# Loads tied in the planner to the up projection also wait for it on the chip

## The chip, the cores and the metric

The kernel runs on one core of one Trainium2 chip. The metric is device time in microseconds (us) of one execution, the median of several.

## What is computed

Two layers, one after the other. The first is a cross-covariance attention over channels: q and k (4 batches, 6208 rows, 256 channels) are normalised along the rows, `kn^T qn` gives a 256 x 256 matrix for each batch, and its softmax multiplies v. The second is a channel mix with a squared relu and a gate.

```python
def _attn_ref(q, k, v, tau):
    qn = q / (np.linalg.norm(q, axis=1, keepdims=True) + 1e-06)
    kn = k / (np.linalg.norm(k, axis=1, keepdims=True) + 1e-06)
    s = kn.transpose(0, 2, 1) @ qn / tau
    a = np.exp(s - s.max(-1, keepdims=True))
    a /= a.sum(-1, keepdims=True) + 1e-09
    return v @ a

def _moe_ref(x, mu_k, mu_r, w_k, w_v, w_r):
    x_prev = np.concatenate([zeros, x[:, :-1, :]], axis=1)
    xk = mu_k * x + (1.0 - mu_k) * x_prev
    xr = mu_r * x + (1.0 - mu_r) * x_prev
    k = np.maximum(xk @ w_k, 0.0)
    v = k * k @ w_v
    r = 1.0 / (1.0 + np.exp(-(xr @ w_r)))
    return r * v
```

Inputs and output are float32; the kernel multiplies in bfloat16.

## The kernel before, in words

**Blocks.** The rows are cut into 48 blocks of 512 (12 for each batch) and one block "left" of the 4 x 64 rows that remain; the constant T = 9.6 us is the planned time of a block. Around the blocks of batch b - 1 the kernel gathers the covariance of batch b: 12 groups of 512 rows of q and k and one small group of 64 rows (32 KB for each of q and k). Only the first batch's covariance comes before all blocks, in a head of some 45 us.

**One block.** A load on POOL's queue brings v as bfloat16 (L394, "ld v"; six buffers `v_bf`); SP's queue turns it with a transposing DMA (L400; six buffers `vT`), or, for the first five blocks, TensorE does. TensorE makes x from `vT` and the softmaxed matrix `A` (L489), ACT takes it out of PSUM into `xR` (L501), and DVE makes `xk` and `xr` (L533, L540, L549). The up projection is four *pairs* (L578): each pair is two planner steps called "up", with two matmuls of 512 columns in each; ACT's relu (L581) and DVE's square (L583) take the pair on. The gate (L611) and the down projection (L616) go to PSUM `vr`, ACT's tanh (L620) and DVE's product (L622) write `res`, of which there are three buffers, and SP stores 512 KB (L636).

**One group of the next covariance.** Two loads on POOL's queue bring q and k (L676, "ld qk"; 13 buffers `qk`); ACT squares them (L691), DVE adds the squares up (L694 to L704), TensorE multiplies (L714). At the end of a batch stand the sums of the squares (L724, L731), a power step on POOL (L277), a chain of small DVE steps (L279 to L296, with matmuls at L302) and the softmax (L433 to L454).

**What sets the order.** Nothing is scheduled by the compiler: `Plan` holds every step with its engine, a cost, a key and the steps it depends on, and `order()` runs a list schedule with these costs. The steps are then emitted in the planned order, and each engine and queue keeps that order on the chip. What an instruction waits for on the chip is set by the tiles that it reads and writes.

**The pace of the loads.** Near the end of the kernel all loads of v and of q and k are sorted by when they are used, and spread at four for each T, at most 3 T ahead of their use. `after_pair(t)` finds the up pair planned for that time:

```python
def after_pair(t):
    at = [m for m in [marks.get((n, p)) for n, p in [divmod(int((t + T) / T * 4), 4)]] if m]
    return at
```

The second "up" step of a pair is its mark (`marks[n, p]`, set in `up_pair`). The load takes the mark as `after=`, and `add` puts it among the load's dependencies. That holds in the planner's time alone: load and matmul share no tile, so on the chip the load waits for its buffer to come free, for one of the DMA queue's semaphores, and for the instructions before it on POOL. Besides the loads, POOL's queue holds a small memset of `xR` at the start of each batch (L473) and the power steps (L277).

Of the kernel before, what the change touches and what calls it, by code (L numbers as in the profile page):

```python
# [15 lines left out]


class Step:
    __slots__ = ("eng", "occ", "lat", "out", "key", "fn", "deps", "users", "left", "ready", "start", "seq", "size", "name", "take", "give")


class Plan:

# [10 lines left out]
        self.readers = {}  # L36
        self.fill_from, self.fill_to, self.fill, self.fill_stop = 0.0, 0.0, None, ()

    def add(self, eng, cost, key, fn, reads=(), writes=(), size=0, name="", after=(), take=None, give=None):
        s = Step()  # L40
        s.occ, s.lat = cost if isinstance(cost, tuple) else (cost, cost)
        s.eng, s.key, s.fn, s.size, s.name = eng, key, fn, size, name
        s.seq = len(self.steps)
        s.take, s.give = take, give
        s.deps, s.users = set(after), []
        for r in reads:
            if r in self.writer:
                s.deps.add(self.writer[r])
            self.readers.setdefault(r, []).append(s)
        for w in writes:  # L50
            if w in self.writer:
                s.deps.add(self.writer[w])
            for r in self.readers.get(w, ()):
                s.deps.add(r)
            self.writer[w] = s
            self.readers[w] = []
        s.deps.discard(s)
        self.steps.append(s)
        return s

    def order(self):
        import heapq
        for s in self.steps:
            s.left = len(s.deps)
            s.ready = 0.0
            for d in s.deps:
                d.users.append(s)
        free = {e: 0.0 for e in self.HOP}
        waiting = {e: [] for e in self.HOP}
        able = {e: [] for e in self.HOP}  # L70
        lanes = {"SP": [], "POOL": []}
        bus = {"SP": 0.0, "POOL": 0.0}
        for s in self.steps:
            if s.left == 0:
                heapq.heappush(waiting[s.eng], (0.0, s.seq, s))
        done = []
        held, queued, open_at = set(), {}, {}
        while True:
            best = None
            for e in free:  # L80
                if able[e]:
                    t = free[e]
                elif waiting[e]:
                    t = max(free[e], waiting[e][0][0])
                else:
                    continue
                if best is None or t < best[0]:
                    best = (t, e)
            if best is None:
                break  # L90
            t, e = best
            if e == "PE" and self.fill and free[e] < self.fill_to and t > self.fill_from and t - free[e] > 0.3:
                at = max(free[e], self.fill_from)
                n = min(512, int((t - at - 0.05) * 2400) // 64 * 64)
                if n >= 64:
                    f = Step()
                    f.eng, f.occ, f.lat = "PE", n / 2400 + 0.0025, n / 2400
                    f.start, f.seq, f.name, f.fn = at, 0, "fill", (lambda n=n: self.fill(n))
                    f.deps, f.users, f.key, f.size, f.out = set(), [], 0, 0, at + f.lat
                    f.take = f.give = None  # L100
                    done.append(f)
                    free[e] = at + f.occ
                    continue
            while waiting[e] and waiting[e][0][0] <= t:
                _, q, s = heapq.heappop(waiting[e])
                heapq.heappush(able[e], (s.key, q, s))
            s = heapq.heappop(able[e])[2]
            if s.take:
                if s.take in held:
                    queued.setdefault(s.take, []).append(s)  # L110
                    continue
                if open_at.get(s.take, 0.0) > t + 1e-9:
                    heapq.heappush(waiting[e], (open_at[s.take], s.seq, s))
                    continue
                held.add(s.take)
            if s.size:
                lane = lanes[e][-8] + 0.25 if len(lanes[e]) >= 8 else 0.0
                if lane > t + 1e-9:
                    heapq.heappush(waiting[e], (lane, s.seq, s))
                    continue  # L120
            s.start = t
            if s.name in self.fill_stop:
                self.fill_to = 0.0
            free[e] = t + s.occ
            end = t + s.lat
            if s.size:
                at, took = max(bus[e], end + self.MOVE), s.size / self.RATE
                if e == "SP" and bus["POOL"] > at:
                    bus["POOL"] += took
                    took *= 4 if s.name == "turn v" else 2  # L130
                bus[e] = at + took
                end = bus[e] + self.LAND
                lanes[e].append(end)
                if t > self.SPARE_FROM:
                    end += self.SPARE
            s.out = end
            if s.give:
                held.discard(s.give)
                open_at[s.give] = end + self.HOP["PE"]
                for w in queued.pop(s.give, ()):  # L140
                    heapq.heappush(waiting[w.eng], (max(w.ready, open_at[s.give]), w.seq, w))
            done.append(s)
            for u in s.users:
                r = free[e] if u.eng == e and not s.size else end + self.HOP[u.eng]
                u.ready = max(u.ready, r)
                u.left -= 1
                if u.left == 0:
                    heapq.heappush(waiting[u.eng], (u.ready, u.seq, u))
        done.sort(key=lambda s: (s.start, s.seq))
        return done  # L150
# [18 lines left out]
def kernel(  # L169
# [104 lines left out]
    def inverse(i, key, srcn, sres, lo, hi, name):  # L274

        nres = ("nq" if lo == 0 else "nk", i)
        add("POOL", (0.8, 0.9), key + .01, lambda: nc.gpsimd.tensor_tensor(nrm[i][:, lo:hi], srcn[:, lo:hi], half[:, lo:hi], op=OP.pow),  # L277
            reads=[(sres, i)], writes=[nres], name=name + " pow")
        add("DVE", TINY, key + .02, lambda: nc.vector.tensor_scalar_add(nrm[i][:, lo:hi], nrm[i][:, lo:hi], 1e-6),  # L279
            reads=[nres], writes=[nres], name=name)  # L280
        rw = [("rrq", i)] if hi == 2 else [("rrk", i)] if lo == 2 else [("rrq", i), ("rrk", i)]
        add("DVE", TINY, key + .03, lambda: nc.vector.reciprocal(rr[i][:, lo:hi], nrm[i][:, lo:hi]),
            reads=[nres], writes=rw, name=name)
        if inv_tau != 1.0 and hi == 4:
            add("DVE", TINY, key + .03, lambda: nc.vector.tensor_scalar_mul(rr[i][:, 2:4], rr[i][:, 2:4], inv_tau),
                reads=[("rrk", i)], writes=[("rrk", i)], name=name)
# [101 lines left out]
    head_last = plan.steps[-1]  # L388


    def v_load(n, key, after=()):
        b, t = blocks[n]
        i = n % NV
        add("POOL", 0.75, key, lambda: nc.gpsimd.dma_start(  # L394
            v_bf[i], v[b, t * M:(t + 1) * M, :].rearrange("(s p) c -> p s c", p=P)),
            writes=[("v_bf", i)], size=M * C * 4, name="ld v", after=after)

    def v_turn_dma(n, key):
        i, o = n % NV, n % NT
# [168 lines left out]
    def up_pair(n, p, c0, c1, w, ku):  # L568
        def go():
# [3 lines left out]
            for x in range(2):  # L573
                fh = 2 * p + x

                def mm(fh=fh, x=x):
                    for dh in range(2):
                        nc.tensor.matmul(kT[bk][:, x, :w], w_k[:, dh, fh * P:(fh + 1) * P], xk[n % 2][:, dh, c0:c1],  # L578
                                         start=dh == 0, stop=dh == 1)
                marks[n, p] = add("PE", pe(w, 2), ku + x * .02, mm, reads=[("w_k",), ("xk", n % 2, c0)], writes=[("kT", bk, x)], name="up")  # L580
            add("ACT", act(2 * w), ku + .1, lambda: nc.scalar.activation(kr[kri][:, :, :w], kT[bk][:, :, :w], AF.Relu, scale=0.5 ** 0.5),  # L581
                reads=[("kT", bk, 0), ("kT", bk, 1)], writes=[("kr", kri)], name="relu")
# [64 lines left out]
    def left_stage(b, key):  # L647
        i = b % 2
        unit(key, lambda: add("POOL", 0.6, key, lambda: nc.gpsimd.dma_start(vl[i][:80], v[b, N - 80:, :]),
                              writes=[("vl", i)], size=80 * C * 4, name="ld v", after=[marks[NB * b + 1, 3]]))  # L650
        unit(key + .1, lambda: add("SP", 1.2, key + T, lambda: nc.sync.dma_start_transpose(vlT[i], vl[i][:80, :]),
                                   reads=[("vl", i)], writes=[("vlT", i)], size=80 * C * 4, name="turn v"))

# [16 lines left out]
    def qk_load(b, g, key, pace):  # L670
# [3 lines left out]
        G = qk[gi]  # L674
        for x, t in enumerate((q, k)):
            add("POOL", 0.55, key + x * .001, lambda x=x, t=t: nc.gpsimd.dma_start(G[:rows, x, :n], src(t, b, g)),  # L676
                writes=[("qk", gi, x, j) for j in range(S)], size=rows * n * C * 4, name="ld qk", after=pace(x))

    def cov_group(b, g, key, dk):
        rows, n = (P, S) if g < NB else (L, 1)  # L680
# [142 lines left out]
        fn()  # L823
    seq = plan.order()
    tc_plan[:] = seq
    for s in seq:
        s.fn()


tc_plan = []  # L830
# [38 lines left out]
```

## Time and profile before

| | |
|---|---|
| timed runs | 527.08, 525.74, 523.83 us; median 525.74 |
| the profiled execution's own time | 524.58 us |
| its span, first to last instruction | 522.8 us |
| TensorE busy (PE) | 490.3 us, 94% of the span |
| DVE, ACT, POOL busy | 434.5, 403.4, 102.7 us |
| moved by DMA | 77.36 MB; HBM read 78.71 MB, written 25.43 MB |
| median from issue to landing, v / k / q loads | 9.3 / 10.3 / 10.3 us |
| median from issue to landing, stores / transposes | 4.3 / 6.8 us |

How to read the lines that follow. PE is TensorE's matmuls, PEld its weight loads, DVE VectorE, ACT ScalarE, POOL GpSimd, SP SyncE; SPq is SP's sequencer, which issues transfers. L578 is line 578 of the kernel. In a row of the timeline the first two numbers are start and duration in us, and a bracket tells how long the engine was idle before it and what ended that. A row of a 10 us stretch gives the busy time of PE, PEld, DVE, ACT and POOL, each with its instructions, then the granted TensorE clock, the DMA share and the GB/s moved. A row of the waits names who waited, for whom, the total in us, how many times, and the longest. A row of the DMA issues ends with the median time from issue to landing. The row of digits "DMA" is the busy share of the DMA engines in 40 equal slices of the span, in tenths.

### The profile page before, as it was taken

The page shows a single profiled execution, that of the slowest core. Times are in us where ns is not written, and L with a number is a line of the kernel's source. Part 1 is how long each engine was busy: PE and PEld are TensorE (multiplying, and loading weights), DVE is VectorE, ACT ScalarE, POOL GpSimd, SP SyncE. Part 2 cuts the span into 40 slices and gives each one's busy share as a digit, 9 for nine tenths or more (in the row PEclk, how much of TensorE's full clock was granted, in tenths as well). Part 3 has the DMA queues.
Part 4 walks back from the last instruction along what each step waited for, and adds up shares of the span by engine and source line. Part 5 has one row for each costly group of instructions (what it writes and reads, how often), then busy time and mean ns, then how long its engine had stood idle before and what let it go on. Part 6 is the DMA issues. An engine that isn't in the chain of part 4 may idle for free.

```text
span 522.8 us, 9475 instructions
## 1 busy us (share of the span) xinstructions
PE 490.3 (94%) x3483; PEld 335.4 (64%) x3544; DVE 434.5 (83%) x988; ACT 403.4 (77%) x576; POOL 102.7 (20%) x174
## 2 busy tenths in 40 slices
PE   1889999999999997999999999999999999999995
PEld 0555666666666674666666667676666666666674
DVE  3768999999989995899779989989669787878973
ACT  4956798988888885788878788888666777777763
POOL 6465433100343321100234211000122000000000
PEclk9999999999999999999999999999999999999999
DMA  9999999993899999942699999642399463322213
GB/s 203 209 203 202 190 216 198 201 203 77 147 182 205 184 198 200 189 100 61 121 203 200 216 165 201 113 107 60 83 161 163 101 105 101 81 82 61 81 45 97
DMA packets 113942, 77.36 MB, mean 148 GB/s; under 512 B 49572, under 2 KB 101480, under 8 KB 113896
## 3 DMA queue, kind: packets, MB, share of 16 engines
q0 software_dynamic: 41776, 38.84, 49.4%
q1 hardware_dynamic: 72120, 37.92, 33.7%
q8 instruction: 27, 0.44, 0.3%
q14 instruction: 19, 0.16, 0.1%
HBM read 78.71 MB, written 25.43 MB: 199 GB/s over the span
## 4 chain that ended last, share of the span: by engine, by line
PE 66%; DVE 19%; DMA 8%; ACT 3%; issue 2%; POOL 0%; SPq 0%; ACTq 0%; DVEq 0%; POOLq 0%
PE vr L616 25%; PE kT L578 24%; PE vr L611 6%; PE xp L489 6%; DMA qk<-in_k_dram 5%; PE s_ps L714 4%; DVE kk L583 4%; DMA out_dram<-res 3%; DVE dm L540 3%; DVE res L622 2%; DVE xk L549 1%; DVE t L694 1%; DVE xr L549 1%; DVE dl L533 1%; ACT kr L581 1%
## 5 line engine op out<-in xcount | busy, mean ns | idle before, releaser
L581 ACT ACTIVATE kr<-kT 128x1024 bf16<-128x1024 f32 (+1 forms) x200 | 200.0, 1002 | 55.1 <-PE kT L578 49.9
L616 PE MATMUL vr<-w_v,kk 128*128 128x256 bf16 x1552 | 204.7, 273 | 1.8 <-DVE kk L583 1.5
L578 PE MATMUL kT<-xk,w_k 128*128 128x512 bf16 (+1 forms) x742 | 200.5, 372 | 5.3 <-DVE xk L549 2.1
L583 DVE TENSOR_TENSOR kk<-kr 128x1024 bf16<-128x1024 bf16 (+1 forms) x200 | 133.6, 670 | 43.8 <-ACT kr L581 43.6
L616 PEld LDWEIGHTS <-kk 128*128 128x128 bf16 x1552 | 150.7, 98 | 24.5 <-DVE kk L583 5.2
L578 PEld LDWEIGHTS <-w_k 128*128 128x128 bf16 x800 | 77.3, 98 | 56.5 <-issue 3.5
L620 ACT ACTIVATE res<-vr 128x256 f32<-128x256 f32 x194 | 75.1, 388 | 22.2 <-PE vr L616 13.5
L622 DVE SCALAR_TENSOR_TENSOR res<-res,vr 128x256 f32<-128x256 f32 x194 | 80.1, 414 | 7.0 <-ACT res L620 7.0
L611 PE MATMUL vr<-w_r,xr 128*128 128x256 bf16 x388 | 74.1, 273 | 3.3 <-DVE res L622 3.2
L501 ACT CAST xR<-xp 128x512 bf16<-128x512 f32 x94 | 55.4, 590 | 21.1 <-PE xp L489 20.9
L691 ACT ACTIVATE sq<-qk 128x2048 bf16<-128x2048 bf16 (+1 forms) x39 | 70.7, 1812 | 0.0
L540 DVE TENSOR_SCALAR dm<-dl,mu 128x512 bf16<-128x512 bf16 (+1 forms) x200 | 61.7, 347 | 1.0
L611 PEld LDWEIGHTS <-xr 128*128 128x128 bf16 x388 | 37.6, 98 | 38.1 <-issue 4.7
L394 POOL DMA_DIRECT2D v_bf<-in_v_dram x48 | 36.6, 765 | 110.4 <-DMA vT<-v_bf 55.5
L489 PE MATMUL xp<-vT,A 128*128 128x512 bf16 x188 | 56.1, 379 | 0.7 <-DVE A L454 0.2
L714 PE MATMUL s_ps<-qk 128*128 128x256 bf16 (+1 forms) x294 | 55.1, 273 | 0.5 <-DVE e_sb L433 0.4
L714 PEld LDWEIGHTS <-qk 128*128 128x128 bf16 (+1 forms) x294 | 28.4, 98 | 15.3 <-issue 1.1
L549 DVE TENSOR_TENSOR xk<-dm,xR 128x1024 bf16<-128x1024 bf16 (+1 forms) x49 | 33.4, 682 | 1.7
L549 DVE TENSOR_TENSOR xr<-dm,xR 128x1024 bf16<-128x1024 bf16 (+1 forms) x49 | 33.4, 682 | 1.5
L533 DVE TENSOR_TENSOR dl<-xR 128x1024 bf16<-128x1024 bf16 (+1 forms) x49 | 33.0, 674 | 0.1
L309 ACT ACTIVATE sq<-qk 128x1024 bf16<-128x1024 bf16 (+2 forms) x26 | 24.1, 975 | 9.0 <-DMA qk<-in_q_dram 5.6
L489 PEld LDWEIGHTS <-A 128*128 128x128 bf16 x196 | 19.1, 98 | 18.4 <-DVE A L454 1.3
(81 smaller groups left out, 251.1 us busy)
## 6 DMA issues: line engine op xcount, KB each, us to landing
out_dram<-res SPq DMA_DIRECT2D x47, 512.0 KB, 4.3
v_bf<-in_v_dram POOLq DMA_DIRECT2D x48, 256.0 KB, 9.3
qk<-in_k_dram POOLq DMA_DIRECT2D x47, 256.0 KB, 10.3
qk<-in_q_dram POOLq DMA_DIRECT2D x46, 256.0 KB, 10.3
f32s<-in_q_dram SPq DMA_DIRECT2D x2, 512.0 KB, 4.2
vT<-v_bf SPq DMA_TRANSPOSE x43, 6.8
w_k<-in_moe_w_k_dram POOLq DMA_DIRECT2D x1, 512.0 KB, 7.0
w_v<-in_moe_w_v_dram POOLq DMA_DIRECT2D x1, 512.0 KB, 8.8
```

The source lines that it names most:

```text
L489: nc.tensor.matmul(dst, A[b][:, ih, dh * P:(dh + 1) * P], vT[o].rearrange("p (s h) q -> p h s q", h=2)[:, ih, c0 // P:c1 // P, :], start=i ...
L540: unit(km, lambda col=col, dh=dh, c0=c0, c1=c1, km=km, w=w: add("DVE", dve(w, 2.77), km, lambda: nc.vector.tensor_scalar_mul(dm[di][:, dh, ...
L549: nc.vector.tensor_tensor(o[which][:, :, c0:c1], dm[di][:, :, c0:c1], xR[:, :, at + c0:at + c1], op=OP.add)
L578: nc.tensor.matmul(kT[bk][:, x, :w], w_k[:, dh, fh * P:(fh + 1) * P], xk[n % 2][:, dh, c0:c1], start=dh == 0, stop=dh == 1)
L581: add("ACT", act(2 * w), ku + .1, lambda: nc.scalar.activation(kr[kri][:, :, :w], kT[bk][:, :, :w], AF.Relu, scale=0.5 ** 0.5), reads=[("k ...
L583: add("DVE", dve(2 * w, 2), ku + .2, lambda: nc.vector.tensor_tensor(kk[n % 2][:, 2 * p:2 * p + 2, c0:c1], kr[kri][:, :, :w], kr[kri][:, : ...
L611: nc.tensor.matmul(V[:, D:], xr[ri][:, dh, s * P:(s + 1) * P], w_r[:, dh, :], start=dh == 0, stop=dh == 1)
L616: nc.tensor.matmul(V[:, :D], kk[n % 2][:, fh, s * P:(s + 1) * P], w_v[:, fh, :], start=fh == 0, stop=fh == 7)
L620: add("ACT", act(D), kd + .3, lambda: nc.scalar.activation(r[:, s], V[:, D:], AF.Tanh, scale=0.5), reads=[("vr", bk)], writes=[("res", oi, ...
L622: add("DVE", dve(D), kd + .4, lambda: nc.vector.scalar_tensor_tensor(r[:, s], r[:, s], 1.0, V[:, :D], op0=OP.add, op1=OP.mult), reads=[("v ...
L691: add("ACT", act(w), key, lambda: nc.scalar.activation(Q[:rows, :, :n], G[:rows, :, :n], AF.Square), reads=both, writes=sqs, name="sq")
L714: nc.tensor.matmul(s_ps[:, ih, :], G[:rows, 1, s, ih * P:(ih + 1) * P], G[:rows, 0, s, :], start=g == 0 and s == 0 and ih == 0, stop=g == ...
```

## The change

The loads of v (of blocks and of the left rows) and of q and k hand their mark over as `gate=` in place of `after=`. For the planner this is the same dependency. When the program is emitted, each load also gets a real dependency on the last matmul of the marked up step, which becomes a wait on a semaphore of TensorE. To have that matmul at hand, a step keeps the instruction that its function returns, and `mm` returns its last matmul. Apart from that, the planner's cost of the power step goes from 0.8 us (0.9 until its result is there) to 1.0 (1.1).

```diff
-    def add(self, eng, cost, key, fn, reads=(), writes=(), size=0, name="", after=(), take=None, give=None):
+    def add(self, eng, cost, key, fn, reads=(), writes=(), size=0, name="", after=(), take=None, give=None, gate=()):
...
-        s.take, s.give = take, give
-        s.deps, s.users = set(after), []
+        s.take, s.give, s.gate, s.inst = take, give, gate, None
+        s.deps, s.users = set(after) | set(gate), []
...
-        add("POOL", (0.8, 0.9), key + .01, lambda: nc.gpsimd.tensor_tensor(nrm[i][:, lo:hi], srcn[:, lo:hi], half[:, lo:hi], op=OP.pow),
+        add("POOL", (1.0, 1.1), key + .01, lambda: nc.gpsimd.tensor_tensor(nrm[i][:, lo:hi], srcn[:, lo:hi], half[:, lo:hi], op=OP.pow),
...
-    def v_load(n, key, after=()):
+    def v_load(n, key, gate=()):
...
-            writes=[("v_bf", i)], size=M * C * 4, name="ld v", after=after)
+            writes=[("v_bf", i)], size=M * C * 4, name="ld v", gate=gate)
...
                 def mm(fh=fh, x=x):
                     for dh in range(2):
-                        nc.tensor.matmul(kT[bk][:, x, :w], w_k[:, dh, fh * P:(fh + 1) * P], xk[n % 2][:, dh, c0:c1],
-                                         start=dh == 0, stop=dh == 1)
+                        last = nc.tensor.matmul(kT[bk][:, x, :w], w_k[:, dh, fh * P:(fh + 1) * P], xk[n % 2][:, dh, c0:c1],
+                                                start=dh == 0, stop=dh == 1)
+                    return last
...
-                              writes=[("vl", i)], size=80 * C * 4, name="ld v", after=[marks[NB * b + 1, 3]]))
+                              writes=[("vl", i)], size=80 * C * 4, name="ld v", gate=[marks[NB * b + 1, 3]]))
...
-                writes=[("qk", gi, x, j) for j in range(S)], size=rows * n * C * 4, name="ld qk", after=pace(x))
+                writes=[("qk", gi, x, j) for j in range(S)], size=rows * n * C * 4, name="ld qk", gate=pace(x))
...
+    wait = mybir.DependencyInfo(mybir.DependencyClass.Sync, mybir.DependencyReason.DATA)
     for s in seq:
-        s.fn()
+        s.inst = s.fn()
+        for g in s.gate:
+            tc.add_manual_dep(s.inst.ins, g.inst.ins.name, wait, reason="pace")
```

More of the change, by code (lines that the diff above doesn't have):

```diff
@@ L18 @@
 class Step:
-    __slots__ = ("eng", "occ", "lat", "out", "key", "fn", "deps", "users", "left", "ready", "start", "seq", "size", "name", "take", "give")
+    __slots__ = ("eng", "occ", "lat", "out", "key", "fn", "deps", "users", "left", "ready", "start", "seq", "size", "name", "take", "give", "gate", "inst")
 class Plan:
@@ L99, in order @@
                     f.deps, f.users, f.key, f.size, f.out = set(), [], 0, 0, at + f.lat
-                    f.take = f.give = None
+                    f.take, f.give, f.gate, f.inst = None, None, (), None
                     done.append(f)
```

## The prediction

> **What bounds the kernel now.** I read the page's busy shares and slices first, then the stretches of 10 us, then the waits and queues where a stretch falls short.
>
> ```profile
> span 522.8 us, 9475 instructions
> PE 490.3 (94%) x3483; PEld 335.4 (64%) x3544; DVE 434.5 (83%) x988; ACT 403.4 (77%) x576; POOL 102.7 (20%) x174
> PEclk9999999999999999999999999999999999999999
> DMA  9999999993899999942699999642399463322213
> ...
> 190.00:200.00 10.00, 9.81 (x70) 6.79 (x70) 6.83 (x15) 5.44 (x7) 1.81 (x3) 1.00 1.23 178
> 200.00:210.00 10.00, 6.68 (x46) 4.45 (x47) 7.71 (x17) 8.03 (x12) 1.86 (x4) 1.00 1.44 210
> 210.00:220.00 10.00, 9.89 (x70) 6.86 (x70) 9.06 (x21) 8.28 (x12) 1.81 (x3) 1.00 1.22 188
> ```
>
> TensorE is the bound: the clock is granted in full, and from 50 to 510 us nearly every stretch of 10 us has 9.8 to 9.95 us of matmul. So a change of transfers can win only what is missing there. The largest hole is 200 to 210 (6.68 us). The waits from 190 to 212 name it, and SP's timeline shows where it begins:
>
> ```profile
> ACT res L620 <- DMA out_dram<-res: 4.4, 1, 4.4
> DVE res L622 <- ACT res L620: 3.8, 1, 3.8
> PE vr L611 <- DVE res L622: 2.2, 2, 1.4
> ...
> 182.69 0.54 SPq L636 DMA_DIRECT2D out_dram<-res  x1
> 183.33 10.97 SPq L400 DMA_TRANSPOSE vT<-v_bf  x1
> 219.61 1.72 SPq L400 DMA_TRANSPOSE vT<-v_bf  x1
> ```
>
> The store issued at 182.69 landed at 200.31 (its landing event). Three `res` buffers go round, so ACT's tanh of the block three further on waited 4.4 us for it; DVE and TensorE stood behind. A transpose holds SP 10.97 us there and 1.72 us in a calm stretch. The cause is on POOL's queue, of whose rows these matter:
>
> ```profile
> 90.05 0.64 POOL L676 DMA_DIRECT2D qk<-in_k_dram  x1 [0.44 <-DMA qk<-in_k_dram]
> 184.26 0.53 POOL L676 DMA_DIRECT2D qk<-in_k_dram  x1 [0.51 <-DMA v_bf<-in_v_dram]
> 211.25 0.56 POOL L676 DMA_DIRECT2D qk<-in_k_dram  x1
> 255.52 0.11 POOL L473 MEMSET xR<- 128x2 bf16 x1 [43.72 <-DVE xr L549]
> 270.01 1.04 POOL L277 TENSOR_TENSOR nrm<-acc,half 128x4 f32<-128x4 f32 x1 [10.88 <-DVE acc L731]
> ```
>
> I paired the planner's order of before with the trace's rows, engine by engine (both keep one order), and so know for each load the up pair that the plan ties it to. Of 124 tied loads 123 are issued before that pair ends, by 24 us on average and 46 at most: the load at 184.26 belongs behind the pair that ends at 227.65, the one at 211.25 behind 252.07. The loads run in bursts until buffers are full, and POOL then stands 43.72 us. What the bursts do to the queues, as issues and median time to landing, first for 150 to 186, then for 203 to 212, then for 420 to 521:
>
> ```profile
> qk<-in_k_dram POOLq DMA_DIRECT2D x9, 256.0 KB, 13.8
> out_dram<-res SPq DMA_DIRECT2D x3, 512.0 KB, 16.1
> ...
> v_bf<-in_v_dram POOLq DMA_DIRECT2D x2, 256.0 KB, 8.1
> qk<-in_k_dram POOLq DMA_DIRECT2D x2, 256.0 KB, 10.5
> ...
> out_dram<-res SPq DMA_DIRECT2D x11, 512.0 KB, 2.9
> v_bf<-in_v_dram POOLq DMA_DIRECT2D x1, 256.0 KB, 4.1
> vT<-v_bf SPq DMA_TRANSPOSE x5, 3.9
> ```
>
> **The change, part by part.**
>
> *The wait itself.* 124 loads now wait on POOL for TensorE. Up matmuls already signal ACT's relu, so TensorE gets no instruction. The hop: the relu at 185.35 starts 0.03 us after the modelled end of its matmuls (184.29 + 1.03), so I take 0.3 us as its upper bound. It makes each load 0.3 us later at most, which is held against the room of the loads below. Price by itself 0, as POOL is 20% busy.
>
> *What stands behind the waiting load on POOL.* Three memsets and three power steps. The memsets at 255.52 and 375.24 follow loads tied to pairs ending at 252.07 and 366.67, long before DVE releases them; the one at 131.77 follows 130.97, and 130.97 + 0.3 + 0.75 = 132.0 makes it 0.3 us late for a column that is read by the first delta of the next batch, a full 28 us behind it in the plan. The power at 150.31 follows a load freed at 149.14 (149.14 + 0.3 + 0.59 = 150.0: in time). The one at 270.01 follows a load freed at 269.38: 269.38 + 0.3 + 0.58 = 270.3, so up to 0.3 us late. The third follows 386.00 and runs at 389.39: in time. A softmax chain hangs on each power, with TensorE gaps around it; so +0.2 us, bounds 0 and 0.6 (twice 0.3).
>
> *Loads issued later.* This is where it can lose. Whoever waits for a q or k load is ACT's square (L691), in ACT's order, with relu and tanh behind it. From the end of its pair to that square each of the 35 tied full k loads has 8.9 to 18 us, most 9 to 11; the q loads have 10.9 and more. The load with the tightest room of all, 8.3 us, is a 32 KB remainder. So the question is how long a paced load takes. The bounds: 4.1 us (alone) and 13.8 (deep in the burst). Paced loads come some 2.4 us apart. A load needs 1.3 us of the engines (loads alone in the head move 203 GB/s, 262 KB each), a store with its transpose 3.0 (DMA share 0.30 of 430 to 440, where one of each runs). A block of some 9.5 us with 3.9 loads thus asks 3.9 x 1.3 + 3.0 = 8.1 us, 85%. The nearest row is 203 to 212, where loads come three at once beside a store and a transpose: 8.1 to 10.5. Without the burst two of three stand less in line, 1.3 to 2.6 us less: I take 6 to 8. That is inside 8.9, price 0; with 0.2 us for single late ones: +0.2. At the upper end, all landing in 10.5 as the median load of the whole trace does, the k loads would be late by 18 us in sum (some 20 loads, 0.9 each).
>
> The Trainium skill ("DMA: Bandwidth & Descriptors", section "Rules for kernel authors") speaks against this change: issue a DMA early and wait for it late, so that its fixed cost overlaps. The trace agrees only in part: early loads were never waited for after the head, but their burst held the store of 182.69 for 17.6 us. By the rule alone the change would win nothing and lose what lands late.
>
> *v loads.* They have 2 to 12 us before SP turns to their transpose, and some will hold SP by up to about 4 us. Behind the transpose on SP stands the next store, a block (9 us) later; the transposed tile is used 8 to 44 us after it lands, and with shallower queues it lands sooner than the 13 to 21 us of the bursts. Price 0.
>
> *The stall at 200.* Paced, a store should land in 3 to 8 us, under the 13.3 us (182.69 to 195.98, where ACT began to wait) from which it hurts. The hole goes. Its size: 9.95 - 6.68 = 3.3 us by the stretch; 4.15 by the gaps between weight loads from 199.59 to 209 beyond a matmul's own time (1.58, 0.84, 1.05, 0.68). I take 3.5. What is late next is nothing on the transfer side: the other gaps (0.5 at 61 and 67, 1.4 at 296 to 300, 1.4 at 395 to 399, some 1.6 at 274 to 280) name DVE and ACT.
>
> *The planner's power step, 0.8 to 1.0 us.* The trace has 1.04 to 1.13 for four columns. No row shows DVE waiting for it, so the number saves nothing itself; it can shift the order around three batch boundaries, whose gaps sum to about 4.6 us. Bounds -4.6 and +4.6; I take 0, since the order is kept by keys and the shift is 0.2 us.
>
> *Sum* against the profiled execution: 524.58 us (span 522.8 and 1.8 around it) - 3.5 + 0.2 + 0.2 = 521.4. Its 524.58 is 1.2 under the median of the three timed runs (525.74; 523.83 to 527.08); as queue depth may differ from run to run, I carry half of that: **522.0 us**, 0.7% below the median.
>
> **The rivals.**
>
> *A: paced loads land late (slower).* Place: the square's wait for the k load, 35 times. It decides from a landing of 8.9 us on. At 10.5 us 18 us of lateness, of which half to all reaches TensorE (the one ACT wait for a DMA, 4.4 us, cost 3.3 to 4.2): 521.4 + 9 to 18 = 530 to 540, say 535. For it: the DMA engines are 85% asked for, and 8.1 to 10.5 is the nearest row. Against: there three loads came at once.
>
> *B: no gain.* The store stall returns elsewhere, or the time passes to the next wait, or the wait does not hold since the last reader of the buffer is later anyway. For it: only one store stall shows in 520 us. Against: 123 of 124 loads lie ahead of their pair. 524 to 526.
>
> *C: more than the one hole.* Crowding also feeds small gaps, and the new order packs the boundaries better: of the remaining gaps (about 4.6 at boundaries, 3 elsewhere) half go: 521.4 - 3.8 = 517.6. Against: these gaps name DVE, not a DMA.
>
> **How the numbers follow.** Forecast (519.5 to 523.5) 0.5, A 0.12, B 0.2, C 0.18. The range 517.5 to 528 leaves out A and the lowest edge of C. My own range, if the mechanism holds, is 519.5 to 523.5. This kernel's measurement tells about 1% from no change; that is 520.5 and 531.0. Faster by over 1%: all of C and a fifth of the forecast, 0.28. Slower by over 1%: most of A and a stray order, 0.12. Within: 0.60.
>
> **What would show each step.** POOL's rows should wait for "PE kT L578" at nearly every load, 2 to 2.5 us apart, with no gap of 25 to 47 us before the memsets; the DMA slices should fall from 9 to 6 to 8 and stay even. Stores should land in 3 to 8 us and transposes hold SP under 4. The row "ACT res <- DMA out_dram" should vanish and 200 to 210 have 9.8 us of matmul. k loads should land in 6 to 8 us. I am wrong if "ACT sq <- DMA qk" appears with over 3 us in sum, if SP rows wait long for v and stores slip, or if boundary gaps grow by over 2 us.

## The result and the profile after

| | before | after |
|---|---|---|
| median, us | 524.79 (523.39 to 527.08, 4 runs) | 519.81 (519.14 to 519.91, 4 runs) |
| profiled execution, us | 524.58, span 522.8 | 519.91, span 518.0 |

The ratio is 0.9898 [0.9858, 0.9939]: 1.0% faster. In a later comparison on another chip (the last experiment) it was 0.9928 [0.9904, 0.9952]. The predicted 522.0 lay 2.2 us above the first median and 1.7 above the second (520.35), both inside the range.

First the page of the kernel after: span, busy times, and the DMA slices, of which each is 13 us.

```profile
span 518.0 us, 9585 instructions
...
PE 494.4 (95%) x3548; PEld 336.4 (65%) x3548; DVE 432.4 (83%) x988; ACT 403.1 (78%) x576; POOL 102.4 (20%) x174
...
DMA  9999999999999997999997799996764686551213
```

Before, the slices alternated between 9 and 2 to 4 (a burst, then full buffers and no loads); now the first 30 slices, up to 388 us, all lie between 6 and 9. The work is the same (the trace of the kernel before lacks some matmul records, 3483 against 3548; of weight loads it has 3544). The stretches of 10 us of the kernel after, in the columns of the stretches shown before (busy PE, PEld, DVE, ACT, POOL, then the clock, the DMA share, GB/s):

```profile
190.00:200.00 10.00, 10.00 (x75) 7.04 (x73) 8.70 (x19) 9.23 (x13) 2.12 (x4) 1.00 0.85 148
200.00:210.00 10.00, 10.00 (x75) 7.06 (x73) 8.94 (x19) 8.52 (x12) 2.03 (x4) 1.00 0.84 147
270.00:280.00 10.00, 9.25 (x66) 6.11 (x65) 9.75 (x25) 9.19 (x15) 1.49 (x3) 1.00 0.82 117
```

The stretch that had 6.68 us of matmul has 10.00. The DMA share of that stretch fell from 1.44 to 0.84 (it adds up the times of packets that overlap, so it can pass 1), and yet TensorE gets all that it needs. The third row holds a batch boundary; as the kernel after is some 4 us ahead there, the row cannot be set against the same stretch of before, and the boundaries are taken up below.

The waits of the kernel after, POOL's largest (who waited, for whom, total us, times, longest):

```profile
POOL v_bf L395 <- PE kT L579: 145.1, 39, 16.6
POOL qk L678 <- PE kT L579: 70.2, 39, 5.9
POOL qk L678 <- ACT res L622: 42.2, 14, 5.4
```

The first two are the new gate. The third is the gate too, under another name: the wait is put down to the engine whose event came last by the profile, but when the issue of each of the 124 tied loads is held against the modelled end of its up pair, all 124 lie behind it, by 0.30 us in the median (0.30 to 2.11). Before, 123 of 124 lay ahead. The row "ACT res <- DMA out_dram" is gone, and no row "ACT sq L693 <- DMA" appeared.

SP's timeline of the kernel after, around the place where the hole was, and POOL's at a batch boundary:

```profile
205.26 0.38 SPq L638 DMA_DIRECT2D out_dram<-res  x1
205.74 2.43 SPq L401 DMA_TRANSPOSE vT<-v_bf  x1
```

```profile
248.24 0.53 POOL L678 DMA_DIRECT2D qk<-in_k_dram  x1 [1.84 <-PE kT L579]
251.22 0.11 POOL L474 MEMSET xR<- 128x2 bf16 x1 [2.45 <-DVE xr L550]
253.02 0.75 POOL L395 DMA_DIRECT2D v_bf<-in_v_dram  x1 [1.69 <-PE kT L579]
...
265.78 0.53 POOL L678 DMA_DIRECT2D qk<-in_q_dram  x1 [2.25 <-issue]
266.32 1.04 POOL L278 TENSOR_TENSOR nrm<-acc,half 128x4 f32<-128x4 f32 x1
268.23 0.59 POOL L678 DMA_DIRECT2D qk<-in_k_dram  x1 [0.86 <-PE kT L579]
```

Transposes hold SP for about 2 us (at most 3.5; before 11.2), and POOL, which had been idle for 43.72 us before this memset, is idle for 2.45. Issues and median time to landing from 150 to 186, where before k loads had 13.8 and stores 16.1 us:

```profile
q0 software_dynamic: 3264, 3.15, 65.6%
q1 hardware_dynamic: 5814, 2.62, 42.2%
...
out_dram<-res SPq DMA_DIRECT2D x4, 512.0 KB, 5.7
...
qk<-in_k_dram POOLq DMA_DIRECT2D x4, 256.0 KB, 5.5
v_bf<-in_v_dram POOLq DMA_DIRECT2D x3, 256.0 KB, 6.0
```

(The first two rows are the queues: packets, MB, and the packets' time as a share of 16 engines over the window; q0 carries POOL's loads, q1 SP's stores and transposes.)

**Where the time went.** Stores are issued in the same order in both traces, so the issue of the same store tells how far the one is ahead at each place:

| store issued in before at, us | in after at | difference |
|---|---|---|
| 105.22 | 105.43 | +0.2 |
| 156.50 | 156.33 | -0.2 |
| 209.70 | 205.26 | -4.4 |
| 266.31 | 262.01 | -4.3 |
| 300.41 | 296.36 | -4.1 |
| 385.69 | 381.64 | -4.1 |
| 415.71 | 410.90 | -4.8 |
| 519.18 (last) | 514.38 | -4.8 |

From 219 to 266 the difference stays at -4.3, and before the hole it was -0.2: some 4.1 us come from the one hole. The rest lies at the three batch boundaries: 0.4 gained at the first (+0.2 to -0.2), 0.25 lost at the second (-4.30 to -4.05), 0.75 gained at the third (-4.05 to -4.80).

What the boundaries gained is in DVE's steps. The first four rows are of the third boundary before, the last two are the same two DVE steps after:

```profile
390.40 2.27 POOL L394 DMA_DIRECT2D v_bf<-in_v_dram  x3
391.44 0.49 DVE L295 CAST rb<-rd 128x2 bf16<-128x2 f32 x1
393.20 2.29 POOL L394 DMA_DIRECT2D v_bf<-in_v_dram  x3
394.97 0.64 DVE L454 TENSOR_SCALAR A<-e_sb,sm 128x256 bf16<-128x256 f32 x1
...
387.39 0.17 DVE L296 CAST rb<-rd 128x2 bf16<-128x2 f32 x1
390.44 0.35 DVE L455 TENSOR_SCALAR A<-e_sb,sm 128x256 bf16<-128x256 f32 x1
```

Before, the loads kept back by the power step go out in one run of issues on POOL, and a few small DVE steps of the softmax chain take up to three times as long. From its first DVE step after the power step to its last the chain takes 7.22, 7.21 and 6.03 us at the three boundaries before, and 6.75, 6.95 and 5.28 after, where POOL issues 3, 2 and no loads beside it in place of 11, 10 and 7. The three kernels whose bursts were left (before, experiments 2 and 3) all have 6.03 or 6.04 us at the third boundary, the eleven others 5.28 or 5.29. That the issues on POOL stretch the steps is read from this; no run tests it by itself.

### The profile page after: what moved, and what is told of

It reads as the page before. It is cut to its first block, busy times and chain, and to the rows that moved or that the text cites. A ratio compares the mean times of both kernels' runs of the same rounds, so it can differ in the third digit from the quotient of the medians.

```text
span 518.0 us, 9585 instructions
## 1 busy us (share of the span) xinstructions
PE 494.4 (95%) x3548; PEld 336.4 (65%) x3548; DVE 432.4 (83%) x988; ACT 403.1 (78%) x576; POOL 102.4 (20%) x174
## 4 chain that ended last, share of the span: by engine, by line
PE 74%; DVE 15%; DMA 5%; ACT 2%; issue 2%; POOL 0%; ACTq 0%; DVEq 0%; POOLq 0%
PE vr L618 27%; PE kT L579 27%; PE vr L613 7%; PE xp L490 7%; DMA qk<-in_q_dram 5%; PE s_ps L716 5%; DVE kk L585 3%; DVE dm L541 2%; DVE res L624 2%; DVE t L696 1%; DVE xk L550 1%; DVE dl L534 1%; ACT kr L583 1%; DVE xr L550 1%; PE kT L765 1%
## 5 line engine op out<-in xcount | busy, mean ns | idle before, releaser
L579 PE MATMUL kT<-xk,w_k 128*128 128x512 bf16 (+1 forms) x800 | 206.2, 373 | 1.4 <-DVE xk L550 1.4
L693 ACT ACTIVATE sq<-qk 128x2048 bf16<-128x2048 bf16 (+1 forms) x39 | 70.7, 1814 | 0.0
L678 POOL DMA_DIRECT2D qk<-in_q_dram x39 | 20.9, 537 | 101.8 <-ACT res L622 32.5
L678 POOL DMA_DIRECT2D qk<-in_k_dram x39 | 20.9, 535 | 65.8 <-PE kT L579 43.7
```

The lines of the kernel that those rows point to most:

```text
L579: last = nc.tensor.matmul(kT[bk][:, x, :w], w_k[:, dh, fh * P:(fh + 1) * P], xk[n % 2][:, dh, c0:c1], start=dh == 0, stop=dh == 1)
L693: add("ACT", act(w), key, lambda: nc.scalar.activation(Q[:rows, :, :n], G[:rows, :, :n], AF.Square), reads=both, writes=sqs, name="sq")
```

## The experiments

The theory: the gates spread the loads, so no store is held up long enough for ACT to wait for its `res` buffer. Rivals: the gain is the planner's, from the power step's cost (1 and 2 tell); the crowd on the queues costs by itself, in more places than the one store (3 and 7 tell); the gates stand at the edge of being too late (4, 5, 8 and 9 tell). Each kernel was compared with the kernel before on its own chip; times are medians. A number called *weight-load gap* is the time between two weight loads beyond the first one's matmul, summed after 45 us: 12.2 us before, 7.1 after. A matmul that runs at a lower clock counts in it too.

**1. The gates alone**, with the planner's cost of the power step as before:

```diff
-        add("POOL", (1.0, 1.1), key + .01, lambda: nc.gpsimd.tensor_tensor(nrm[i][:, lo:hi], ...
+        add("POOL", (0.8, 0.9), key + .01, lambda: nc.gpsimd.tensor_tensor(nrm[i][:, lo:hi], ...
```

> The gates alone; the power step is planned at 0.8 us as before, so the order of every engine is that of before. Theory (the gates remove one hole, in which ACT waited for a store held up by a burst of loads): 4.2 to 4.4 us off, 520 to 521 us, no row of ACT waiting for a store, no row of a square waiting for a load. Rival R1 (the gain is many small effects of less crowded queues): about the same time, but spread over the span. Rival R2 (the new order from the power step's cost carries the gain): no gain, 524 to 525 us.

Measured: 521.63 us (519.81 to 522.51, and one execution of 531.79), ratio 0.9923 [0.9899, 0.9948]; loads land in 5.9 to 6.4 us, the hole is gone (4.0 us, at the one place), the weight-load gap is 8.0 us. One square waits 0.8 us for its load, where none was expected. The median is a little over the forecast and 1.8 us over the kernel after; the profiled execution (521.32) loses its 1.4 us against after in the head, where the granted clock is 0.50 for 3.4 us from 33.0. So the gates carry the gain.

**2. The power step's cost alone**, on the kernel before (the same line, 0.8 to 1.0):

> The power step's planned cost alone (1.0 us), no gates. The order differs from before only up to about 73 us of the plan. Theory: 524 to 525.5 us, with ACT still waiting 3 to 5 us for a store near 200 us. Rival R1: the same. Rival R2: 520 to 521 us.

Measured: 525.14 us (521.58 to 526.6, 12 runs), ratio 0.9996 [0.9975, 1.0017]. The waits of this kernel still hold the stall:

```profile
ACT res L620 <- DMA out_dram<-res: 7.1, 2, 6.1
```

The number gives nothing by itself. It changes the planned order only in the first 77 us.

**3. A fourth `res` buffer** on the kernel before, without any gate. The burst stays; only whom it hits is taken away.

```diff
-    res = ring("res", 3, [S, D], F32)
+    res = ring("res", 4, [S, D], F32)
...
-        ri, oi = n % 3, n % 3
+        ri, oi = n % 3, n % 4
```

> The kernel before with four res buffers in place of three, nothing else: loads still run in bursts, stores are still late, but tanh no longer waits for them. Same order on every engine. Theory: the hole at 200 us goes although stores still take up to 17 us: 520 to 521 us. Rival R1: the crowding stays and with it most of the loss: 523 to 524.5 us. Rival R2: 524 to 525 us.

Measured: 520.72 us (520.34 to 521.79), ratio 0.9919 [0.9899, 0.9939]. Its stretches, and its issues from 150 to 186:

```profile
190.00:200.00 10.00, 10.00 (x74) 7.06 (x73) 8.65 (x19) 8.99 (x13) 1.81 (x3) 1.00 1.26 194
200.00:210.00 10.00, 10.00 (x74) 6.99 (x73) 9.04 (x19) 8.52 (x12) 1.84 (x3) 1.00 1.42 201
```

```profile
q0 software_dynamic: 4532, 4.64, 82.8%
q1 hardware_dynamic: 5324, 2.42, 33.5%
...
qk<-in_k_dram POOLq DMA_DIRECT2D x9, 256.0 KB, 12.8
...
out_dram<-res SPq DMA_DIRECT2D x3, 512.0 KB, 15.9
```

Loads and stores are as late as before (a store at worst 17.3 us), the DMA share is as high, and TensorE has no hole. So most of what the crowd costs, it costs where ACT waits for a store's buffer, and one more buffer brings nearly what 124 waits bring. The rest is at the batch boundaries, where nothing is gained against before: the softmax chains take 7.13, 7.21 and 6.04 us, and the medians of after and of experiment 7 lie 0.9 and 0.7 us lower.

**4. Every gate one up pair later** (the wait on the chip only; the plan is that of after):

```diff
+    ups = [marks[n, p] for n in range(NBLK) for p in range(4)]
+    place = {id(m): i for i, m in enumerate(ups)}
...
         for g in s.gate:
+            g = ups[min(max(place.get(id(g), 0) + 1, 0), len(ups) - 1)]
```

> The changed kernel with every gate moved one up pair later on the chip (about 2.4 us), the order kept. It measures how much room the paced loads have. The k loads' room from gate to square falls from 8.9 to 10 us to about 6.5 to 7.5, and they land in some 6.5 (median). Theory (the room decides, and it was enough by 2 to 3 us): squares begin to wait for loads, 3 to 12 us in sum, time 521 to 527 us. Rival (ACT's own slack hides it, or room is much wider than I read): no change against the changed kernel, 519.5 to 520.5 us.

Measured: 531.5 us (530.79 to 532.43), ratio 1.0126 [1.0099, 1.0154], some 11.5 us over the changed kernel's 520, where 1 to 7 were expected. A row of its waits, and one of its stretches:

```profile
ACT sq L693 <- DMA qk<-in_k_dram: 7.3, 6, 2.8
```

```profile
270.00:280.00 10.00, 7.98 (x60) 5.17 (x59) 4.42 (x14) 7.83 (x9) 2.32 (x3) 1.00 1.03 172
```

This is rival A of the prediction, brought about by 2.4 us. The k loads land fast (5.9 us in the median), but the room from gate to square has shrunk to 5.7 to 6.4 us at the tightest. The weight-load gap rose by 10.6 us, to 17.7, most of it at batch boundaries (3.6 us at 270 to 280), where the softmax chain hangs on the last square. The six waits are 7.3 us of that. The rest is TensorE's clock:

```profile
157.80:161.20 3.40, 3.40 (x18) 2.30 (x16) 3.33 (x9) 2.01 (x6) 0.59 (x1) 0.50 0.48 58
280.70:284.10 3.40, 3.19 (x16) 2.19 (x16) 3.29 (x11) 1.86 (x5) 0.05 (x1) 0.50 0.57 77
```

Twice, at holes of 1.7 us and more, the granted clock is 0.50 for 3.4 us, and half of the time that matmul takes there, 1.7 and 1.6 us, is lost. 7.3 + 3.3 = 10.6 us is the whole rise; the spans differ by 10.7 (528.7 against 518.0).

**5. Every gate two up pairs earlier** (the same code with - 2):

> The changed kernel with every gate two up pairs (about 4.8 us) earlier, order kept. The squares get 13 us and more of room and the loads stay paced. Theory (the gain is one hole, lateness plays no part in the changed kernel): the same as the changed kernel, 519.5 to 521 us. Rival (the changed kernel still loses something to loads that arrive just in time): 517 to 519 us.

Measured: 529.87 us (528.56 to 535.32), ratio 1.0116 [1.0054, 1.0177]. The theory, more room and the same pace, failed. Its issues from 150 to 186, and its waits:

```profile
q1 hardware_dynamic: 5395, 2.51, 67.9%
q0 software_dynamic: 2889, 2.64, 66.9%
...
out_dram<-res SPq DMA_DIRECT2D x3, 512.0 KB, 14.5
qk<-in_k_dram POOLq DMA_DIRECT2D x4, 256.0 KB, 14.0
...
v_bf<-in_v_dram POOLq DMA_DIRECT2D x3, 256.0 KB, 13.1
vT<-v_bf SPq DMA_TRANSPOSE x4, 21.6
```

```profile
ACT sq L693 <- DMA qk<-in_k_dram: 6.6, 3, 3.6
...
ACT res L622 <- DMA out_dram<-res: 5.1, 3, 3.6
```

Nearly as many loads and stores as in after (14 against 16), paced in the same way, land two to three times as late, from about 140 to 280 us; afterwards all is fast again (mean landing of loads in slices of 20 us from 120: 7.9, 15.6, 12.7, 11.0, 12.8, 12.3, 17.0, 14.7, 6.6). This is not the burst of before: the engines move less, 5.19 MB in the window against 5.80 in after and 7.10 with four `res`, and each packet takes longer. A share times 16 engines times 36 us over the packets gives for q1 0.679 x 576 / 5395 = 72 ns, against 42 in after and 36 with four `res`; for q0 133 ns against 116 and 105. I call this state the jam. Of the 8.8 us that the span is longer than after, a granted clock of 0.50 for 3.4 us from 287.4 makes some 1.6. POOL's timeline suggested how it begins: behind the memset and the power step, loads go out together.

```profile
132.02 0.11 POOL L474 MEMSET xR<- 128x2 bf16 x1 [4.37 <-DVE xr L550]
132.53 0.53 POOL L678 DMA_DIRECT2D qk<-in_q_dram  x1 [0.41 <-ACT kr L583]
133.05 0.54 POOL L678 DMA_DIRECT2D qk<-in_k_dram  x1
```

**6. Gates on the v loads only** (`ld qk` back to `after=pace(x)`):

> Gates on the v loads alone; q and k loads have none and are held only by the v load ahead of them on POOL's queue. Theory (it is enough that no burst gets far ahead, and POOL's order carries the pace): 519.5 to 521.5 us, no wait of ACT for a store, two to three loads together after each v load, landing in 6 to 9 us. Rival (each load must be paced by itself): stores are late again, 522 to 525 us.

Measured: 519.46 us (519.21 to 520.31), ratio 0.9896 [0.986, 0.9931]. The load rows of its costliest groups and of its DMA issues:

```profile
L395 POOL DMA_DIRECT2D v_bf<-in_v_dram x48 | 36.3, 756 | 303.4 <-PE kT L579 291.3
```

```profile
out_dram<-res SPq DMA_DIRECT2D x47, 512.0 KB, 4.3
v_bf<-in_v_dram POOLq DMA_DIRECT2D x48, 256.0 KB, 5.6
qk<-in_k_dram POOLq DMA_DIRECT2D x47, 256.0 KB, 7.9
```

POOL's queue keeps its order, so a q or k load cannot pass the waiting v load: 48 of the 124 gates set the pace of all.

**7. The changed kernel with four `res` buffers** (the diff of 3 on top):

> The changed kernel with four res buffers. Theory (both remove the same hole): nothing is added, 519.5 to 520.5 us. Rival (two different gains): both together, 515.5 to 517 us.

Measured: 519.99 us (519.91 to 520.11), ratio 0.9908 [0.9878, 0.9937]. The two edits do not add up: they close the same hole.

**8. Only the v gates one pair later** (the code of 4 with `+ (s.name == "ld v")`):

> The changed kernel with the gates of the v loads alone one pair later; q and k keep their own gates, though a q load behind a v load waits with it where both have gates near each other. Theory (the loss of the run with all gates one pair later is the squares' wait for k loads): little lost, 519.5 to 521.5 us. Rival (late v loads, through SP's queue or the transposes, carry that loss): 525 us or more.

Measured: 523.16 us (520.97 to 526.74, 10 runs), ratio 0.9977 [0.9951, 1.0003]: between the two expectations. Its waits tell the way:

```profile
ACT sq L693 <- DMA qk<-in_k_dram: 4.4, 2, 2.4
```

The v loads meet the q and k loads of the next pair; from 140 to 160 loads take 11.8 us in the mean and stores 14.8, a short jam, and two squares wait for k. It is the squares again, but through the queues, not through v.

**9. Every gate one pair earlier** (the code with - 1):

> Every gate one up pair earlier than in the changed kernel. In the run with two pairs earlier the transfers fell behind from 132 us on (loads, stores and transposes then took 11 to 23 us until 290 us) although loads were issued at the same pace. Theory (earlier gates let loads gather behind the memset and the power step on POOL, and the engines are so near to full that the heap lasts): with one pair few loads gather, 519.5 to 522 us, landings back at 5 to 8 us. Rival (any earlier gate puts the loads on top of a store and a transpose in each block): about half of the loss, 524 to 526 us, landings over 9 us from 130 us on.

Measured: 519.27 us (518.45 to 519.77), ratio 0.9903 [0.9868, 0.9938], landings of 5 to 7 us, no jam. As fast as the changed kernel.

**10. Two pairs earlier, without the gathering.** If loads that gather behind POOL's memset and power step start the jam, it should go when the three loads behind each keep their own gate:

```diff
+    since = 9
     for s in seq:
+        if s.eng == "POOL":
+            since = 0 if s.name == "xcol" or s.name.endswith("pow") else since + 1
...
+            g = ups[max(place.get(id(g), 0) - (2 if since > 3 else 0), 0)]
```

> Gates two pairs earlier, but the three loads behind each memset and each power step on POOL keep the changed kernel's gates, so that none can gather there. Theory (gathering there starts the jam): 519.5 to 522 us, no stretch with landings over 10 us. Rival (the place of the loads in the block starts it): 527 to 531 us as with all gates two pairs earlier.

Measured, nine executions: 518.91, 519.19, 520.8, 525.76, 528.42, 528.46, 529.51, 530.37, 535.26. The median is 528.42; the ratio of 0.9934 [0.9885, 0.9983] holds for the four shortest alone. The profiled one (528.46) is jammed from about 60 to 200 us, beginning away from those places, and then stores are what hurts:

```profile
ACT res L622 <- DMA out_dram<-res: 12.7, 4, 9.4
```

In the hole that the longest of them leaves, the granted clock falls to 0.50 for 6.8 us (from 194.7), some 2.3 us more. The theory is not borne out: in this execution the jam began without the gathering. One and the same program runs in 519 or in 528 us; that the jam makes the other long ones long was not profiled.

**11. Two pairs earlier, with the stores halved.** Kernel 5, in which the full blocks store only the first half of each partition's rows, so the output is left incomplete:

```diff
-                        add("SP", 0.42, ks, lambda: nc.sync.dma_start(o, r), reads=alls, size=M * D * 4, name="store")
+                        add("SP", 0.42, ks, lambda: nc.sync.dma_start(o[:, :2], r[:, :2]), reads=alls, size=M * D * 4, name="store")
```

> Gates two pairs earlier, and the stores of 47 of the 49 blocks write only half of their rows, so that a block asks the DMA engines for some 0.75 us less; the rest of the output is left out. Theory (the jam lasts because the engines are asked for nearly all that they give): the jam dissolves or does not start, loads land in 5 to 8 us after 200 us, 518 to 522 us. Rival (the jam does not depend on how much is moved): 527 us or more.

Measured: 519.87 us (ten executions: seven from 519.57 to 520.02, then 521.3, 522.0 and 524.76), ratio 0.9931 [0.9906, 0.9956]. Of its DMA issues:

```profile
out_dram<-res SPq DMA_DIRECT2D x49, 256.0 KB, 2.9
...
qk<-in_k_dram POOLq DMA_DIRECT2D x47, 256.0 KB, 5.9
```

With the same early gates and less to move, 10 us of the loss are gone, and the profiled execution (519.66) lands its loads in 7.0 us at most in the mean of any 20 us from 40 us on. So the gates' place is not slow by itself. That the jam needs DMA engines near full fits, but is not shown: by bytes they were not at their most (144 GB/s in the jam, 197 with four `res`), and shorter stores also free SP's queue sooner for the transposes behind them.

**12. The changed kernel once more**, for how steady it is:

> The changed kernel itself, for more executions than the first four (519.1 to 519.9 us). With gates two pairs earlier the same program took 518.9 in one execution and 535.3 in another, and the gates alone took 531.8 once in six. Theory (at its own gates the changed kernel keeps clear of the jam): all executions 518.5 to 521 us. Rival (it stands next to the jam and falls into it by chance): one or more of them over 525 us.

Measured, nine executions: 519.70, 519.72, 519.77, 519.87, 520.35, 520.53, 521.27, 521.44, 525.09; before, on the same chip, 524.72 (523.59 to 526.0, 14). Ratio 0.9928 [0.9904, 0.9952]. The profiled one has no wait of ACT for a store, nor one of the blocks' squares for a load. Eight of nine are at or near 520 (two of them over the 521 of the theory), and the ninth is over the 525 that the rival named: the kernel is not clear of long executions. The ninth was not profiled; its granted clock was 0.992 over the whole, against 0.995 to 1.0 in the others, so part of it is TensorE's clock, and whether a jam stood behind that is open.

## Why the prediction was right, and where it was off

- **The bound and the cause: right.** TensorE bounds the kernel, and the hole at 200 came from a store held up by a burst of loads. Experiment 3 shows the last link by itself: with the burst as it was and one more `res`, the hole is gone; experiment 7 shows that gate and buffer close the same hole.
- **The size of the hole: too small.** The sum went by 3.5 us, between 3.3 from the stretch and 4.15 from the weight-load gaps. The store issues give 4.1. The gaps were the better ruler: the stretch's edge at 200.00 cut off part of the idle time (190 to 200 had 9.81 us), and its yardstick of 9.95 us comes from a trace that lacks some matmul records; a calm stretch of after has 10.00. (Added up, the recorded terms give 521.5, not 521.4.) With 4.1 in place of 3.5 they give 520.9.
- **The wait itself, priced at 0: right.** Loads go out 0.30 us after the pair's modelled end in the median, as the bound said, and nothing depends on it.
- **Behind the waiting load on POOL: right within its bounds.** The power step of the second boundary ran at 266.32, the moment the load ahead of it was out, as foreseen: 3.7 us earlier than before (270.01), while the work around it was 4.3 us earlier, so 0.6 us late, the upper bound. The chain behind it began 0.45 us late and was 0.26 us shorter, and the store issues lose 0.25 us there, near the +0.2.
- **Loads issued later: right, and tighter than it looks.** k loads landed in 5.9 us in the median of the tied full ones (9 of 10 within 8.1, worst 9.4), against 6 to 8 forecast, and none was late, so the second +0.2 was not needed. The smallest slack between a landing and its square was 1.06 us. Experiment 4 shows rival A at work when 2.4 us of room are taken. The 85% of the engines is not a filling level: it adds bytes at the head's rate for the loads to a DMA share for the store, and that share reached 1.44 at 200 to 210.
- **v loads, the power step's cost: 0 was right** (a transpose holds SP for 3.5 us at most; experiment 2). The bounds of 4.6 us for the planner's number were put at the wrong place: the order at the batch boundaries does not change, only that of the head.
- **The rivals.** B is out. C holds in part: the boundaries gave 0.4 + 0.75 - 0.25 = 0.9 us, not 3.8. Against C the prediction held that these gaps name DVE and not a DMA; they do, but DVE itself was slower beside the burst's issues on POOL. A is a neighbour: its place was right, and the waits cost about their length, as priced; on top came 3.3 us of a halved clock, which the prediction did not have. Nothing in the prediction foresaw the other edge, gates that are too early (5 and 10): between one pair too late and two pairs too early there are two places, 0 and - 1, and both are good. That the change stands on one of them was luck as far as the early edge goes.
- **The rule set against the change.** To issue early and wait late, the rule in the Trainium skill ("DMA: Bandwidth & Descriptors", "Rules for kernel authors"), pointed the wrong way here: loads up to 46 us early cost some 4 us through a store, and loads some 5 us early (experiment 5) cost 10, most of it through a jam. It holds as far as the room to the first use: 2.4 us too late cost 11.5.

Read from the store issues, the span goes from 522.8 us to 522.8 + 0.2 (the head) - 0.4 - 4.1 + 0.25 - 0.75 = 518.0, the span that was measured. These terms are read from the same pair of traces, so the sum describes and does not confirm.

## What to carry to other kernels

Where a planner paces transfers, look whether anything on the chip holds that pace: pair the planned order with the trace and count the transfers that run ahead. Then follow a burst to whom it hurts, since the crowd apart from that cost only some 1 us here; a second edit that frees only the victim (one more output buffer) tells the cause and may be the cheaper cure. Where a wait seems to cost more than its length, read the granted clock behind it. Where many transfers share the queues, try the gate one step to both sides before keeping it, and time it more than a few times.

## What the runs showed of the hardware that was not expected

- **A jam that lasts.** Paced loads, stores and transposes can fall into a state in which all land two to three times as late for some 140 us (loads 5 to 6 against 11 to 17 us, stores 6 against 15, transposes 7 against 20), with less moved (144 against 161 GB/s) and longer packets (72 against 42 ns on SP's queue). Going by the times, the same program met it in some executions and missed it in others (518.91 to 535.26 us), and halved stores kept most clear of it; one execution of each was profiled. In the one start that I followed (experiment 10) a load issued at 58.47 landed at 69.64, and nothing landed between 63.67 and 68.05 while the first transpose was under way. What starts it stays open.
- **A burst is not a jam.** With loads up to 46 us ahead the same engines moved 197 GB/s, and k loads landed in 12.8 us (experiment 3), with packets of 36 ns on SP's queue against 72 in the jam.
- **A transposing DMA's hold on SP follows the crowd**: 1.7 to 3.5 us paced, up to 11.2 us in the burst, with the next store behind it.
- **A halved clock at a hole.** In six of the traces TensorE's granted clock is 0.50 for 3.4 or 6.8 us long before the kernel's end: twice in experiment 4, once each in 1, 2, 3, 5 and 10. Each time TensorE had fallen idle for 1 us or more 1.8 to 4.5 us earlier. Before has a hole of 1.4 us at 200 us and after one of 1.2 in the head without it; what decides was not tested.
- **DVE steps beside load issues.** Two DVE steps of the third softmax chain took 0.49 and 0.64 us while POOL issued seven loads one after the other, and 0.17 and 0.35 us where it issued none. Others beside the same issues kept their length (the cast at 391.04 in before, 0.17 us).
